# Segmented memory attention with a routed MLP: first step and tail rearranged, scratch layout of the left sums changed

## The chip, the cores and the metric

The kernel runs on one core of one Trainium2 chip. The metric is the device time of one launch in microseconds (us); less is better. The engines have short names: PE (matrix multiply, with PEld for its weight loads), DVE (vector), ACT (scalar), POOL (GpSimd) and SP (sync, which here only issues transfers). SBUF is the on-chip memory of 128 partitions, PSUM the small memory into which PE writes.

## The reference

x has 2048 rows of 1024, S = 64 segments of 32 rows; 32 heads of 128; F = 3584.

```python
xn = _layernorm(x)
mem = mem0                                      # 8 rows
for s in range(n_seg):
    xs = xn[:, s * seg_len:(s + 1) * seg_len, :]
    h = concatenate([mem, xs], axis=1)          # 40 rows
    q, k, v = h @ Wq, h @ Wk, h @ Wv            # 32 heads of 128
    p = softmax(where(mask, q @ k.T * E ** -0.5, -1e9))
    o = (p @ v) @ Wo                            # 40 rows of 1024
    mem = o[:, :M, :]                           # the next segment's memory
    outs.append(o[:, M:, :])
r = xn @ w_r; idx = argsort(-r)[:, :2]          # two routed rows
y = (silu(xn[idx] @ w_gate) * (xn[idx] @ w_up)) @ w_down * sigmoid(r[idx])
return x + concatenate(outs) + xn + scatter(y at idx)
```

## The kernel before

**Steps.** The 64 segments follow each other, since the memory of one is the output of the one before; each is a step. A segment of 40 rows is split into 32 *main* rows (8 memory and 24 own rows), whose products are made in its step, and 8 *left* rows, its last ones. The left rows need no memory for their q, k and v: the first step (s = 0) makes these for all segments at once (`left_qk`, `left_v`), with the matmul L500 into `PSG` and L527 into `PSV`, copies them into `GA` and `VG` and stores them to DRAM (`ql_d`, L519, and `vl_d`, L531). The later steps load their part back. The sums of the left rows (`OTL`) go to DRAM in every step (`ol_d`, stored by `store_sums`, L604) and are turned into output rows for all segments in the tail, by `load_left_out` (L595) and `left_rows_out` (matmul L874).

**Weights.** Wq, Wk, Wv and Wo are 64 granules of 512 KB, 0 to 47 in six phases of eight (Wq, Wk of heads 0 to 15, then of 16 to 31, then Wv), 48 to 63 Wo. 44 stay in SBUF (`wres`, `XLT`, `W8A`, `W8B`, `HP`), 3 are kept in PSUM, 17 are streamed in each step through five slots (`g`). A slot comes free when the matmuls on its granule are done. In the first step they come from the inputs; POOL's copies (`wsc`) are their source from step 1 on. Some resident granules come late, since their place first holds something else: `v_homes` are the places of Wv granules, and the last of them (`hx`) holds the router's scratch `XR` and the blocks `VG`.

**Phases of a step.** PE makes q and k of the main rows (L745), transposes them (L632), scores (L650, L652), after two more phases v, P V (L703, L706) and Wo (L798) into `WO`; DVE copies `WO` to `XN` (L828), which ends the step. In the first step, `left_qk` stands behind phases 0 to 3 and `left_v` behind 4 and 5.

**The router**, in the first step: row statistics on DVE (L238 to L242), square root on ACT (L243), `spread` on PE (L250) brings mean and scale of each row to its place, then `router_tile` for 16 tiles of 128 rows on DVE (L263, L265), and `router_out`, a top-2 over all rows, and the routed rows' numbers. `QKL` (L513), the first left q and k that the first step itself needs, is copied by DVE, then `KT` by ACT (L640) and DVE (L642).

**The tail.** `left_rows_out(0)`, `gate_up` for the first 20 of 32 pieces, `left_rows_out(1)`, `gate_up` for the rest, silu (L920), product (L922), the down matmuls (L930) into `YP`, and one sum (L933) with the two routed rows of the output. Since all rows of the output are stored without y before that, POOL loads these two rows back (L916) and SP stores them (L936), at row numbers that are read from memory. In `gate_up` each 128 x 128 block of w_gate or w_up is the stationary operand and the two rows (`RXT`) are the moving one: 14 blocks x 32 pieces = 448 matmuls with 2 columns.

**Order.** The program's order on each engine is the order in which the source writes it; an engine takes its instructions strictly in that order. SP and ACT share eight semaphore lanes for their transfers (DMAHW0 to 7), POOL has eight of its own (DMASW0 to 7); they are given out in turn, and a transfer waits for the one before it on its lane. Waits between instructions go by the tile that they read or write.

Of the kernel before, what the change touches and what calls it, by code (L numbers as in the profile page):

```python
# [22 lines left out]
KEPT_HERE = (FIRST_KEPT, NEXT_KEPT, HALF_KEPT)  # L23
NEG = -30000.0
# [5 lines left out]
def kernel(  # L30
# [29 lines left out]
    FH = F // 2  # L60
    SCALE = float(E) ** -0.5
# [56 lines left out]
    ol_d = [dram.tile([16, P, XL * H], BF16, name=f"ol_d{t}") for t in range(4)]  # L118
# [142 lines left out]
    def router_tile(t):  # L261
        XR = home(hx, [P, D], BF16, "XR")
        nc.vector.tensor_scalar(out=XR[:, :], in0=xt(t), scalar1=RI16[:, t, 0:1], scalar2=RI16[:, t, 1:2],  # L263
                                op0=ALU.subtract, op1=ALU.mult)
        nc.vector.tensor_tensor_reduce(out=XR[:, :], in0=XR[:, :], in1=WRB, scale=1.0, scalar=0.0,  # L265
                                       op0=ALU.mult, op1=ALU.add, accum_out=RF[:, t:t + 1])
# [155 lines left out]
    flow += [(s, g) for s in range(NSEG) for g in (streamed if s else first_streamed)]  # L422
# [6 lines left out]
    def fetch_moe(n=64):  # L429
        while moe and free_homes and n:  # L430
# [9 lines left out]
            else:  # L440
                nc.sync.dma_start(out=t.rearrange("p (a d) -> p a d", a=2),
                                  in_=B_w_down[2 * what[1] * P:(2 * what[1] + 2) * P, :].rearrange("(a p) d -> p a d", a=2))
# [35 lines left out]
    for g in range(KC, 32):  # L478
        if g in first_streamed:
# [6 lines left out]
    for g in v_homes[8:-1]:  # L486
# [6 lines left out]
    def left_qk(mat, half, Gs, between, h0=0, h1=16):  # L493
# [15 lines left out]
        if mat == 1:  # L509
# [3 lines left out]
            nc.vector.tensor_copy(out=qkl[0][:, half].rearrange("p m i q r -> p (m i q r)"), in_=G3[:, 0, :])  # L513
# [7 lines left out]
    def left_v(half, Gs):  # L521
        VG = home(hm, [P, 2048], BF16, "VG")
        for b in range(4):
            for jq in range(4):
                PSV = psA.tile([P, 512], F32, tag="acc", name="PSV")
                for kc in range(KC):
# [4 lines left out]
                nc.sync.dma_start(out=vl_d[b][4 * jq:4 * jq + 4, :, :, half, :].rearrange("i s r e -> (s r) i e"),  # L531
                                  in_=VQ.rearrange("p (i e) -> p i e", i=4))
# [15 lines left out]
    def left_done(p):  # L548
        for g in range(8 * p, 8 * (p + 1)):
            if g in first_streamed:  # L550
                fetch()
        if p == 1:
# [41 lines left out]
    def load_left_out(k, queue):  # L594
        queue.dma_start(out=areas["big0"][:, 4 * k:4 * k + 4, :], in_=ol_d[k // 4][4 * (k % 4):4 * (k % 4) + 4].rearrange("s p c -> p s c"))  # L595
# [6 lines left out]
    def store_sums():  # L602
        s, t = unsaved.pop(0)
        nc.gpsimd.dma_start(out=ol_d[s // 16][s % 16], in_=t.rearrange("p r h -> p (r h)"))  # L604
# [367 lines left out]
```

## Time and profile before

| | us |
|---|---|
| median of three runs | 1859.54 |
| lowest, highest | 1859.37, 1860.27 |
| the profiled execution | 1847.92 |
| its span | 1846.3 |
| first step, to the last copy of WO (L828) | 241.4 |
| 63 later steps, to 1760.3 | 1518.9 |
| tail | 86 |

Over the span PE is busy 84%, DVE 48%, ACT 42%, POOL 17%; 678.5 MB are moved at 367 GB/s in the mean. The table has three parts that are limited in different ways: the first step makes the left rows of all segments, the later steps each bring in 17 granules (8.9 MB), and the tail makes the left rows' outputs and the routed MLP. An order in time has a row for each run of like instructions: start, duration, engine, line, operation, out<-in, and in brackets the idle time of the engine before it and what ended it.

### The profile page before, as it was taken

To read this page: it belongs to the slowest core of one execution; us is meant where nothing else is said; L and a number is where in the kernel's file an instruction comes from. 1 tells how busy PE (TensorE), PEld (TensorE's weight loads), DVE (VectorE), ACT (ScalarE), POOL (GpSimd) and SP (SyncE) were. 2 spreads that over 40 slices of the span, in tenths; PEclk is the share of its full clock that TensorE was granted. 3 is DMA by queue.
4 is the path that set the end of the run, shared out by engine and by line. 5 is a ranking of instruction groups with operands and counts; after the bars stand their busy time and mean duration, and the time that the engine had idled before them with its cause. 6 is when DMAs were issued, how large, how long until landed. Compare 5 with 4: busy or idle time off the path is not lost. (4 is left out here: it accounts for less than half of the span.)

```text
span 1846.3 us, 70379 instructions
## 1 busy us (share of the span) xinstructions
PE 1555.7 (84%) x30358; PEld 828.2 (45%) x30370; DVE 880.4 (48%) x2711; ACT 774.9 (42%) x2019; POOL 320.9 (17%) x592
## 2 busy tenths in 40 slices
PE   6889978888888888888888888888888888888888
PEld 3334434444444444444444444444444444444465
DVE  6631235555554454555555555444455555555420
ACT  2333134444444444444444444444444444444400
POOL 1020111111111111111111111111111111111200
PEclk9999989999999999999999999999999999999988
DMA  9684899999999999999999999999999999999996
GB/s 361 218 301 135 261 367 391 393 394 394 368 387 376 368 389 383 392 386 372 396 393 396 396 394 394 385 386 389 386 391 394 397 382 393 395 395 395 392 364 251
DMA packets 223288, 678.50 MB, mean 367 GB/s; under 512 B 46848, under 2 KB 54320, under 8 KB 222976
## 3 DMA queue, kind: packets, MB, share of 16 engines
q1 hardware_dynamic: 196768, 623.79, 88.3%
q0 software_dynamic: 24192, 46.54, 7.5%
q8 instruction: 237, 3.88, 0.8%
q10 hardware_dynamic: 2016, 3.67, 0.6%
q14 instruction: 75, 0.61, 0.1%
HBM read 652.90 MB, written 29.89 MB: 370 GB/s over the span
## 5 line engine op out<-in xcount | busy, mean ns | idle before, releaser
L745 PE MATMUL PSm<-wres,ST 128*32 128x512 bf16 x6400 | 500.7, 382 | 0.0
L745 PEld LDWEIGHTS <-ST 128*32 128x32 bf16 x12288 | 313.3, 96 | 349.5 <-issue 107.4
L745 PE MATMUL PSm<-g,ST 128*32 128x512 bf16 x3084 | 307.3, 384 | 46.6 <-DMA g<-wsc 38.2
L411 ACT COPY BK<-KEPT 128x512 bf16<-128x512 bf16 x315 | 189.3, 601 | 175.0 <-PE WO L798 65.1
L798 PEld LDWEIGHTS <-OT 128*32 128x32 bf16 x8192 | 209.2, 97 | 85.6 <-issue 69.3
L754 ACT CAST XB<-PSm 128x512 bf16<-128x512 f32 x256 | 150.2, 587 | 132.7 <-PE PSm L745 131.1
L642 DVE COPY KT<-BT 128x512 bf16<-128x512 bf16 x128 | 51.8, 405 | 290.6 <-PE BT L632 290.6
L798 PE MATMUL WO<-W8B,OT 128*32 128x256 bf16 x4096 | 186.2, 276 | 0.0
L745 PE MATMUL PSm<-W8A,ST 128*32 128x512 bf16 x2048 | 182.7, 380 | 0.0
L587 POOL DMA_DIRECT2D QKL<-ql_d x63 | 46.5, 738 | 755.7 <-ACT OTL L714 740.6
L798 PE MATMUL WO<-g,OT 128*32 128x256 bf16 x2560 | 130.7, 277 | 53.1 <-DMA g<-wsc 48.8
L832 POOL DMA_DIRECT2D out_dram<-XN x256 | 130.7, 526 | 173.9 <-DVE XN L828 173.8
L779 ACT CAST VM<-PSm 128x512 bf16<-128x512 f32 x128 | 80.3, 627 | 114.0 <-PE PSm L745 114.0
L411 DVE COPY BK<-KEPT 128x512 bf16<-128x512 bf16 x189 | 80.2, 425 | 72.3 <-ACT BK L411 36.9
L632 PEld LDWEIGHTS <-XB 128*128 128x128 bf16 x1024 | 57.9, 98 | 106.6 <-ACT XB L754 101.5
L674 DVE TENSOR_REDUCE DN<-BS 128x8 f32<-128x320 f32 x128 | 62.9, 491 | 88.0 <-ACT BS L669 88.0
L632 PE MATMUL BT<-IDENT,XB 128*128 128x128 bf16 x1024 | 101.7, 222 | 3.1
L500 PE MATMUL PSG<-XLT,wres 128*128 128x512 bf16 x352 | 101.3, 390 | 0.8 <-ACT GA L502 0.7
L637 ACT COPY QT<-BT 128x512 bf16<-128x512 bf16 x128 | 74.9, 585 | 53.4 <-PE BT L632 51.4
L659 DVE TENSOR_TENSOR BS<-BS,CT 128x96 f32<-128x96 f32 (+1 forms) x256 | 59.7, 233 | 76.5 <-PE BS L652 72.0
L745 PE MATMUL PSm<-BK,ST 128*32 128x512 bf16 x567 | 76.7, 388 | 22.2 <-DVE ST L369 22.2
L828 DVE CAST XN<-WO 128x256 bf16<-128x256 f32 x64 | 27.2, 424 | 127.5 <-PE WO L798 127.5
(171 smaller groups left out, 2278.9 us busy)
## 6 DMA issues: line engine op xcount, KB each, us to landing
g<-wsc SPq DMA_DIRECT2D x1071, 512.0 KB, 6.3
ql_d<-GA POOLq DMA_DIRECT2D x16, 512.0 KB, 6.3
QKL<-ql_d POOLq DMA_DIRECT2D x63, 128.0 KB, 6.2
MW<-in_B_w_gate_dram SPq DMA_DIRECT2D x16, 448.0 KB, 8.0
MW<-in_B_w_down_dram SPq DMA_DIRECT2D x14, 512.0 KB, 8.3
wres<-in_A_Wk_dram SPq DMA_DIRECT2D x12, 512.0 KB, 10.5
MW<-in_B_w_up_dram SPq DMA_DIRECT2D x12, 448.0 KB, 8.5
XP<-in_A_x_dram SPq DMA_DIRECT2D x8, 512.0 KB, 10.1
```

The costliest lines, as they stand in the source:

```text
L411: copy(out=back[g][c], in_=KEPT_COLS[g][c])
L500: nc.tensor.matmul(PSG[:, :], lhsT=part(Gs[kc], h // 4)[:, P * (h % 4):P * (h % 4 + 1)], rhs=XLT[:, :, kc, :], start=(kc == 0), stop=(kc = ...
L632: nc.tensor.transpose(out=PTq[:, il, :, :].rearrange("p j r -> p (j r)"), in_=XB[:, il * P:(il + 1) * P], identity=IDENT[:, :])
L637: nc.scalar.copy(out=QT[half][:, :, :], in_=pv)
L642: nc.vector.tensor_copy(out=KT[half][:, :, 0:32], in_=pv)
L659: nc.vector.tensor_tensor(out=S4, in0=S4, in1=m, op=ALU.add)
L674: nc.vector.tensor_reduce(out=DN[:, :], in_=S8, axis=AX.X, op=ALU.add)
L745: nc.tensor.matmul(PSm[32 * jq:32 * jq + 32, :], lhsT=ST[:, kc, :], rhs=part(Gv, jq), start=(kc == 0), stop=(kc == KC - 1), tile_position= ...
L754: nc.scalar.copy(out=XB[:, :], in_=PSm[:, :])
L779: nc.scalar.copy(out=VM[half][:, :], in_=PSm[:, :])
L798: nc.tensor.matmul(PS[32 * g:32 * g + 32, 0:256], lhsT=lhs(h), rhs=Gv[:, D * hs + 256 * g:D * hs + 256 * (g + 1)], start=False, stop=(last ...
L832: nc.gpsimd.dma_start(out=out2[s * SEG:s * SEG + XM, 256 * g:256 * (g + 1)], in_=OB[32 * g:32 * g + XM, :])
```

## The change

It has five parts.

1. *Guest granule.* Granule 15 (phase 1) is loaded by SP among the first resident ones, into the place of granule `v_homes[8]`, and not into a stream slot; `v_homes[8]` itself is loaded after phase 1.
2. *Router.* Square root, `spread` and the 16 router tiles stand behind the left block of phase 0 instead of inside that of phase 1; `XR` has two buffers. The copies of `QKL`, and of `KT` in the first step, are made by ACT instead of DVE.
3. *Stores of v.* The stores of the last two left v blocks of half 1 are issued by POOL instead of SP.
4. *Layout of ol_d.* Partition first, segment second, so a store writes 512 B rows 8 KB apart, and a load of four segments reads 2 KB rows.
5. *Tail.* gate and up have the two rows, padded to 32 columns (`RX`), as the stationary operand and 448 columns of the weights as the moving one, in four column tiles: 128 matmuls. The result has rows of F over the partitions, so it is transposed (7 transposes) behind silu and product, and w_down is loaded in another row order. Silu's table is loaded ahead by an activation of one column. `keep_warm` puts 12 and 5 matmuls with no use into PE's pauses. The left rows' stores go to POOL (three) and SP (the last) instead of ACT, the two routed rows' stores to SP and ACT.

```diff
-    ol_d = [dram.tile([16, P, XL * H], BF16, name=f"ol_d{t}") for t in range(4)]
+    ol_d = [dram.tile([P, 16, XL * H], BF16, name=f"ol_d{t}") for t in range(4)]
...
+    def router_tiles():
+        XR = home(hx, [P, 2, D], BF16, "XR")
+        for t in range(NT):
+            nc.vector.tensor_scalar(
+                out=XR[:, t % 2, :], in0=xt(t), scalar1=RI16[:, t, 0:1], scalar2=RI16[:, t, 1:2],
+                op0=ALU.subtract, op1=ALU.mult)
...
-    moe += [("dn", fg) for fg in range(FC // 2)]
+    moe += [("dn", j, gp) for j in range(FC // 4) for gp in range(2)]
...
+        if g == GUEST:
+            t = res_tiles[g] = room(v_homes[8], "guest")
+            nc.sync.dma_start(out=t, in_=granule_dram(g))
...
-            nc.vector.tensor_copy(out=qkl[0][:, half].rearrange("p m i q r -> p (m i q r)"), in_=G3[:, 0, :])
+            nc.scalar.copy(out=qkl[0][:, half].rearrange("p m i q r -> p (m i q r)"), in_=G3[:, 0, :])
...
-                nc.sync.dma_start(out=vl_d[b][4 * jq:4 * jq + 4, :, :, half, :].rearrange("i s r e -> (s r) i e"),
-                                  in_=VQ.rearrange("p (i e) -> p i e", i=4))
+                (nc.gpsimd if half and b > 1 else nc.sync).dma_start(
+                    out=vl_d[b][4 * jq:4 * jq + 4, :, :, half, :].rearrange("i s r e -> (s r) i e"), in_=VQ.rearrange("p (i e) -> p i e", i=4))
...
     def left_done(p):
...
-        if p == 1:
+        if p == 0:
+            sd_rows(MV[:, 1:NT, :], VE[:, 1:NT])
+            spread(1, NT)
+            router_tiles()
+        elif p == 1:
+            res_tiles.pop(GUEST)
+            load_resident(v_homes[8])
...
-                nc.vector.tensor_copy(out=KT[half][:, :, 0:32], in_=pv)
+                (nc.vector.tensor_copy if s else nc.scalar.copy)(out=KT[half][:, :, 0:32], in_=pv)
...
-                        sd_rows(MV[:, 1:NT, :], VE[:, 1:NT])
-                        left_qk(mat, half, Gs, kept, 1, 3)
-                        h1 = 3
-                        spread(1, NT)
-                        for t in range(NT):
-                            router_tile(t)
...
+    def keep_warm(n):
+        W = psK.tile([P, 512], F32, name="WARM", tag="kept0")
+        for i in range(n):
+            nc.tensor.matmul(W[:, 0:256], lhsT=IDENT[:, :], rhs=T2[:, 256:512], start=True, stop=True)
...
-            nc.scalar.dma_start(out=out2.rearrange("(t s r) d -> t s r d", t=4, s=16)[2 * k + b, :, XM:SEG, :], in_=x)
+            (nc.sync if k and b else nc.gpsimd).dma_start(
+                out=out2.rearrange("(t s r) d -> t s r d", t=4, s=16)[2 * k + b, :, XM:SEG, :], in_=x)
...
-            for fl in range(FC // 2):
-                col = (w * FC + fh * (FC // 2) + fl) * 2
-                nc.tensor.matmul(GU[:, col:col + 2], lhsT=Gt[:, fl * P:(fl + 1) * P], rhs=RXT[:, kc, :],
-                                 start=(w + kc + fh + fl == 0), stop=True, skip_group_check=True)
+            for g in range(4):
+                nc.tensor.matmul(GU[w][fh][32 * g:32 * g + 32, 0:FQ], lhsT=RX[:, kc, :], rhs=Gt[:, FQ * g:FQ * (g + 1)],
+                                 start=(kc == 0), stop=(kc == KC - 1), tile_position=(0, 32 * g), skip_group_check=True)
...
-    SG = T2[:, 64:64 + 4 * FC].bitcast(F32)
-    nc.scalar.activation(out=SG, in_=GU[:, 0:FC * 2], func=ACTF.Silu)
-    HT = T2[:, 256:256 + 2 * FC].rearrange("p (f c) -> p f c", c=2)
-    nc.vector.tensor_tensor(out=HT.rearrange("p f c -> p (f c)"), in0=SG, in1=GU[:, FC * 2:FC * 4], op=ALU.mult)
+    HR = T0[:, 256:256 + 2 * FQ]
+    SG = [[T0[:, 1152 + 448 * i:1152 + 448 * (i + 1)].bitcast(F32) for i in range(2)],
+          [one.tile([P, 224], F32, tag=tag, name="SG") for tag in ("bA", "bE")]]
+    for fh in range(2):
+        for i in range(2):
+            nc.scalar.activation(out=SG[fh][i], in_=GU[0][fh][:, 224 * i:224 * (i + 1)], func=ACTF.Silu)
...
+    keep_warm(12)
+    HTP = psA.tile([P, 1024], BF16, tag="acc", name="HTP")
+    for j in range(FC // 4):
+        nc.tensor.transpose(out=HTP[:, P * j:P * (j + 1)], in_=HR[:, P * j:P * (j + 1)], identity=IDENT[:, :])
...
+    keep_warm(5)
...
-        v = nc.sync.value_load(I8[0:1, c:c + 1], min_val=0, max_val=S - 1)
-        nc.sync.dma_start(out=routed_out(v), in_=quarters(c))
+        ends[c].dma_start(out=routed_out(end_rows[c]), in_=quarters(c))
```

The first step on ACT, around the left block of phase 1 (`GA` is a left block's copy, `MISC` holds the row statistics, L243 is the square root), before:

```order
L502 CAST GA<-PSG 128x64x8 [waits PE_49] x2
L637 COPY QT<-BT 128x512 [waits PE_49]
L754 CAST XB<-PSm 128x512 [waits PE_49]
L502 CAST GA<-PSG 128x64x8 [waits PE_49]
L243 ACTIVATE MISC<-MISC 128x15 [waits DVE_49]
L502 CAST GA<-PSG 128x64x8 [waits PE_49] x15
L640 COPY KT<-QKL 128x16x8 [waits DVE_49,PE_49]
```

and in the change:

```order
L515 CAST GA<-PSG 128x64x8 [waits PE_49] x2
L245 ACTIVATE MISC<-MISC 128x15 [waits DVE_49]
L656 COPY QT<-BT 128x512 [waits DVE_49,PE_49]
L773 CAST XB<-PSm 128x512 [waits PE_49]
L515 CAST GA<-PSG 128x64x8 [waits PE_49] x16
L526 COPY QKL<-GA 128x256 [waits DMASW3_49,DMASW2_49,DMASW4_49,DMASW1_49,Activation_49]
L659 COPY KT<-QKL 128x16x8 [waits PE_49,Activation_49]
L661 COPY KT<-BT 128x16x32
```

The square root has moved ahead of the copy of phase 1's q, and the two copies ahead of the scores stand on ACT itself.

SP at the end of the first step, from the last v stores on, before (`XLT` and `wres` take resident Wo granules, `wsc` is the stream of step 1):

```order
L531 DMA vl_d_100<-VG 128x4x128 [waits DMAHW3_49,Activation_49]
L531 DMA vl_d_100<-VG 128x4x128 [waits DMAHW4_49,DVE_49]
L386 DMA g<-in_A_Wo_dram 128x2x1024 [waits DMAHW5_49,PE_49]
L386 DMA g<-in_A_Wo_dram 128x2x1024 [waits DMAHW6_49,PE_49]
L386 DMA g<-in_A_Wo_dram 128x2x1024 [waits DMAHW7_49,PE_49]
L136 DMA XLT<-in_A_Wo_dram 128x2x1024 [waits DMAHW0_49]
L136 DMA wres_2055<-in_A_Wo_dram 128x2x1024 [waits DMAHW3_49,DMAHW2_49,DMAHW4_49,DMAHW1_49,Pool_49]
L388 DMA g<-wsc_105 128x2048 [waits PE_49]
```

and in the change:

```order
L544 DMA vl_d_98<-VG 128x4x128 [waits DMAHW2_49,DVE_49]
L138 DMA XLT<-in_A_Wo_dram 128x2x1024 [waits DMAHW3_49,PE_49]
L559 DMA VL<-vl_d_97 128x1x128 [waits DMAHW6_49,DMAHW5_49,DMAHW4_49]
L390 DMA g<-in_A_Wo_dram 128x2x1024 [waits PE_49] x2
L390 DMA g<-in_A_Wo_dram 128x2x1024 [waits DMAHW7_49,PE_49]
L138 DMA XLT<-in_A_Wo_dram 128x2x1024 [waits DMAHW0_49]
L138 DMA wres_2040<-in_A_Wo_dram 128x2x1024 [waits DMASW3_49,DMASW2_49,DMASW4_49,DMASW1_49,DMASW7_49,DMASW0_49,DMAHW1_49,DVE_49,DMAHW2_49,Activation_49,Pool_49]
L392 DMA g<-wsc_105 128x2048 [waits PE_49]
```

Eight stores have left this place; the load into wres, whose place held VG, waits for the landings on POOL's lanes as well.

ACT in the tail, before (`T_39898` is T2, `GU` the sums of gate and up):

```order
L881 DMA out_dram<-XLS 16x8x1024 [waits DMAHW2_49,DVE_49]
L920 ACT_TABLE_LOAD [waits PE_49]
L920 ACTIVATE T_39898<-GU 128x56 [waits Activation_49]
```

and in the change (`T_39883` is T2, `T_39888` is T0, into which POOL loads the two routed rows on lanes DMASW2 and DMASW3):

```order
L935 ACT_TABLE_LOAD
L935 ACTIVATE T_39883<-T_39883 128x1 [waits Activation_49]
L942 TENSOR_LOAD CT [waits DVE_49]
L942 ISA x2
L948 ACTIVATE T_39888<-GA_40055 128x224 [waits DMASW3_49,DMASW2_49,PE_49]
L948 ACTIVATE T_39888<-GA_40055 128x224
L948 ACTIVATE SG<-GA_40056 128x224 [waits PE_49]
L948 ACTIVATE SG<-GA_40056 128x224
```

The first silu of the change waits for two of POOL's lanes besides PE.

More of the change, by code (lines that the diff above doesn't have):

```diff
@@ L23 @@
 KEPT_HERE = (FIRST_KEPT, NEXT_KEPT, HALF_KEPT)
+GUEST = 15
 NEG = -30000.0
@@ L60 @@
     FH = F // 2
+    FQ = F // 8
     SCALE = float(E) ** -0.5
@@ L485 @@
             load_x(g - 7)
-    for g in v_homes[8:-1]:
+    for g in v_homes[9:-1]:
         load_resident(g)
@@ L892, in routed_out @@
         return out2[bass.ds(v, 1), :].rearrange("o (g d) -> (o g) d", g=4)
-    GU = psA.tile([P, 512], F32, tag="acc", name="GU")
+    ends = (nc.sync, nc.scalar)
+    GU = [[psA.tile([P, 512], F32, tag="acc", name=f"GA{fh}") for fh in range(2)], [BS, BT]]
+    RX = T2[:, 256:512].rearrange("p (k r) -> p k r", r=32)
+    nc.vector.memset(T2[:, 256:512], 0.0)
+    nc.vector.tensor_copy(out=RX[:, :, 0:2], in_=RXT)
     pieces = [(w, kc, fh) for w in range(2) for kc in range(KC) for fh in range(2)]
```

52 lines of the change are left out of this document (31 added, 21 removed).

## The prediction

> **What bounds the kernel now.** I read the stretches of the span first, then the order in time of the engines in the two stretches that the change touches. The columns are the stretch, its length, busy time (and instructions) of PE, PEld, DVE, ACT and POOL, the granted clock, the DMA share and GB/s.
>
> ```profile
> 0.00:61.00 61.00, 40.51 (x284) 20.90 (x284) 37.77 (x97) 17.47 (x30) 4.75 (x19) 0.98 0.99 372
> 61.00:130.00 69.00, 62.27 (x341) 27.12 (x341) 34.85 (x66) 19.89 (x36) 12.38 (x24) 0.92 0.69 239
> 130.00:228.00 98.00, 92.37 (x567) 41.76 (x569) 21.38 (x47) 30.00 (x56) 15.54 (x30) 1.00 0.63 199
> 265.60:1737.00 1471.40, 1238.13 (x27402) 661.25 (x27406) 745.46 (x2383) 684.04 (x1835) 273.17 (x494) 1.00 1.01 389
> 1760.00:1846.00 86.00, 76.52 (x810) 52.16 (x814) 16.24 (x40) 2.99 (x4) 3.25 (x6) 0.86 0.86 307
> ```
>
> The middle, four fifths of the span, moves weights at a DMA share of 1.01: no compute saving shows there. From 61 to 228 us the DMA share is 0.63 to 0.69 and PE is busy nine tenths: there PE's waits set the time, and what they lose is lost for good, because every later step streams at a fixed rate. The tail from 1760 us is a chain on PE. So I price the first step and the tail as chains, the middle as bytes.
>
> **First step: guest granule and router.** Two stalls of PE stand in phases 1 and 2.
>
> ```profile
> 51.98 0.33 SPq L386 DMA_DIRECT2D g<-in_A_Wk_dram  x1
> 53.44 0.18 DVE L242 TENSOR_SCALAR MISC<-MISC 128x15 bf16<-128x15 bf16 x1
> 60.73 0.62 PE L745 MATMUL PSm<-g,ST 128*32 128x512 bf16 x4 [5.54 <-DMA g<-in_A_Wk_dram]
> 61.28 1.46 PE L500 MATMUL PSG<-XLT,wres 128*128 128x512 bf16 x3
> 65.39 0.22 ACT L243 ACTIVATE MISC<-MISC 128x15 bf16<-128x15 bf16 x1
> 69.80 0.45 DVE L263 TENSOR_SCALAR XR<-XP,MISC 128x1024 bf16<-128x1024 bf16 x1
> 97.54 0.55 DVE L263 TENSOR_SCALAR XR<-XP,MISC 128x1024 bf16<-128x1024 bf16 x1
> 78.01 0.81 PE L500 MATMUL PSG<-XLT,wres 128*128 128x512 bf16 x3
> 78.88 0.81 PE L500 MATMUL PSG<-XLT,wres 128*128 128x512 bf16 x3
> 91.06 1.05 PE L745 MATMUL PSm<-wres,ST 128*32 128x512 bf16 x16
> 99.58 0.30 ACT L640 COPY KT<-QKL 128x128 bf16<-128x128 bf16 x1 [7.83 <-DVE QKL L513]
> 99.93 0.23 PE L650 MATMUL BS<-KT,QT 128*32 128x40 bf16 x4 [6.73 <-ACT KT L640]
> 100.75 2.25 PE L500 MATMUL PSG<-XLT,wres 128*128 128x512 bf16 x5
> ```
>
> The first stall is granule 15: its load is issued at 51.98, when a stream slot comes free, and PE waits 5.54 us for it. Then PE runs at half pace for a while: three matmuls take 1.46 us, where from 78.01 to 78.88 four start in 0.87 (one of another tile stands between), 0.216 each. The left block after the stall lasts 29.8 us (61.28 to 91.06) against 27.6 at the steady pace (16 heads of 8, 128 x 0.216): 2.2 more. The guest loads the granule some 20 us sooner into a place that nobody reads before phase 4; the resident granule of that place is loaded after phase 1, at a DMA share of 0.69. What is not removed is the new place of spread: its four matmuls on PE wait for ACT's square root, which by 53.44 has its input but stands behind ACT's copy of a left block, and then runs at about 54.0; about 1.1 us of PE. Gain 5.54 + 2.2 - 1.1 = **6.6**.
>
> The second stall is the router on DVE: its 16 tiles start at 69.80 and come every 1.85 us ((97.54 - 69.80) / 15); the copy of QKL stands behind them, ACT waits 7.83 for it, PE 6.73 for ACT. Started at about 55.3 instead, the tiles end at 84.9, when phase 2 is just beginning at 84.5 (91.06 less the 6.6); its scores come about 2 us later, and the QKL and KT copies stand on ACT by now. The wait becomes the copies' own 0.25. With the half-paced start of the block behind it (the five at 100.75 take twice their 1.08, the four before them 0.35 too much: 1.4) the gain is 6.73 + 1.4 - 0.25 = **7.9**. The same KT copy on ACT costs 0.3 at phase 4. If the router's DVE work had no cover in phase 1's wait for data, its 29.6 us would have to stand somewhere else; DVE is busy 34.85 of 69 us there, so it has room.
>
> **First step: stores of the v blocks.**
>
> ```profile
> 215.07 14.52 SPq L531 DMA_DIRECT2D vl_d<-VG  x8
> 228.51 0.69 DVE L530 CAST VG<-PSV 128x512 bf16<-128x512 f32 x1 [3.82 <-DMA vl_d<-VG]
> 229.68 2.44 SPq L386 DMA_DIRECT2D g<-in_A_Wo_dram  x3
> 232.91 0.37 SPq L136 DMA_DIRECT2D wres<-in_A_Wo_dram  x1
> 234.04 0.62 PE L798 MATMUL WO<-g,OT 128*32 128x256 bf16 x8 [2.81 <-DMA g<-in_A_Wo_dram]
> 227.00:232.00 5.00, 3.79 (x92) 2.57 (x91) 2.68 (x11) 1.22 (x5) 0.39 (x2) 1.00 0.47 108
> 232.00:241.00 9.00, 4.63 (x66) 2.30 (x65) 0.44 (x2) 0.46 (x2) 0.50 (x1) 0.53 1.04 391
> ```
>
> Eight stores hold SP for 14.52 us, since each waits for its copy; three Wo granules, one more into XLT and the last resident one (wres) queue behind them. PE then waits 2.81, and less three times more, and the DMA share is 0.47 in 227 to 232. With the stores on POOL's queue the four granules can be issued about 5 us sooner. But wres goes where the VG blocks stand, so it still waits for the landing of POOL's last stores, and the stream of step 1 stands behind it on SP. POOL has only the eight W8B loads beside them. Lower bound: the idle DMA time of that stretch alone, 5 x 0.53 = 2.7 us. Upper: SP free at 223 to 224 instead of 229.6, about 6.5. Since wres can go only 1.5 us sooner, but finds the four loads done (2.1 MB, 5.4 us at 391 GB/s, half of it in idle time), I take **4**. First step in all: 6.6 + 7.9 - 0.3 + 4 = **18.2**, bounds 14 to 22.
>
> **Steady steps: layout of ol_d.** Each step stores 64 KB. Before, it was one contiguous block; now rows of 512 B stand 8 KB apart. The rows on q1 are those of 100 us of the steady part, of SP's loads of 512 B pieces (1787 to 1794), and of 1.5 us with 256 B stores (204.5 to 206).
>
> ```profile
> q1 hardware_dynamic: 10342, 37.66, 96.6%
> q1 hardware_dynamic: 2646, 2.39, 109.6%
> q1 hardware_dynamic: 1448, 0.37, 107.9%
> ```
>
> A big packet takes 0.966 x 16 x 100 / 10342 = 149 ns, a 256 B one 1.079 x 16 x 1.5 / 1448 = 18 ns. 64 KB are 16 big packets (2.4 us of engine time) or, at the worst of these, 256 small ones (4.6): 2.2 / 16 = 0.14 us a step, 8.6 in all. The mix of 512 B pieces moves 2.39 MB in 7.67 engine-shares-us against 37.66 in 96.6, which makes 0.21 instead of 0.17 us for 64 KB: 2.6 in all. I take **-3**, bounds -8.6 and 0. The loads of ol_d at the end get 2 KB rows instead; worth 0.5.
>
> **Tail.**
>
> ```profile
> 1790.02 1.28 DVE L880 TENSOR_TENSOR XLS<-XLS,WD 128x512 bf16<-128x512 bf16 x2 [10.84 <-PE WD L874]
> 1797.54 1.39 PE L903 MATMUL GU<-RXT,MW 128*128 128x2 bf16 x47 [1.31 <-issue]
> 1814.51 7.07 PE L874 MATMUL WD<-W8B,OTA 128*128 128x512 bf16 x32
> out_dram<-XLS ACTq DMA_DIRECT2D x4, 256.0 KB, 6.4
> T<-out_dram POOLq DMA_DIRECT2D x2, 2.0 KB, 2.5
> 1830.43 2.24 PE L903 MATMUL GU<-RXT,MW 128*128 128x2 bf16 x84
> 1832.75 1.28 ACT L920 ACT_TABLE_LOAD   x1 [58.68 <-PE GU L903]
> 1834.29 0.21 DVE L922 TENSOR_TENSOR T<-T,GU 128x56 bf16<-128x56 f32 x1 [4.55 <-ACT T L920]
> 1834.88 5.80 PE L930 MATMUL YP<-MW,T 128*2 128x256 bf16 x112 [2.22 <-DVE YP L924]
> 1835.79 1.21 POOL L916 DMA_DIRECT2D T<-out_dram  x2 [73.17 <-DMA out_dram<-XLS]
> 1840.74 0.48 DVE L933 SCALAR_TENSOR_TENSOR T<-YP,SIG,T 128x256 bf16<-128x256 f32 x1 [5.91 <-PE YP L930]
> 1835.00:1840.50 5.50, 5.50 (x112) 3.50 (x104) 0.00 (x0) 0.00 (x0) 1.21 (x2) 0.53 0.02 4
> ```
>
> The first pass of left rows ends at 1790.2. gate_up now needs RX, which DVE writes behind its adds: 1790.02 + 1.28, a memset and a copy of about 0.2 each, so it starts 1.5 us later than now. It then is 448-column matmuls in four column tiles, 0.19 us per group (the steady step runs four of 512 in 0.217): 20 groups 3.8, where 8.75 stood, 12 groups 2.3 for 4.2. The second pass of left rows runs 128 x 0.2155 = 27.6, without its slow start (29.55). The end of gate_up moves from 1832.7 to 1825.4, and the table load of 1.28 stands before it: **7.3 + 1.3 in hand**.
>
> I don't count it. The silu and its product now write into T0, the tile into which POOL loads the two routed rows, and both carry a wait for those two loads: other columns, but the wait is on the tile. Before, they wrote T2 and waited for nothing of the kind; only the last sum (L933) did. The rows can be loaded when all left rows are stored: the last adds end at 1824.5, the store lands 5.5 to 6.4 later (1830 to 1831), two issues (1.21) and a landing of 2.5 make about **1834**, where the silu ran at 1834.04 before. Behind it now stand four silus and products (1.6), seven transposes (0.4) and five warming matmuls at half pace (1.0), beside which the HT copy and the memset of YP run: 3.0 us, against 0.84 before (1834.04 to 1834.88). The down matmuls start at about 1837 instead of 1834.88. The pause that the 12 warming matmuls were to fill has grown to some 8 us, so PE is slow again and the 5.8 stay. Tail: -2.1 + 0.5 for ol_d, **-1.6**; bounds -4 and +1.
>
> The last row of the fence bears on that pace: in 5.5 us without a gap the clock is 0.53. The Trainium skill ("TensorE: Matmul & The Clock Gate", Part 1: The HAM clock gate) says that half rate follows an idle window of some 3.4 us and full rate some 3.4 us of sustained work. By that the five warming matmuls and the first down ones would release the clock and the down block would last about 4.1, an estimate; the trace disagrees, it has half pace for 5.5.
>
> **Sum.** 18.2 - 3 - 1.6 = 13.6 us. The profiled execution took 1847.92 with a span of 1846.3; the median of the runs is 1859.54, 11.6 above. 1847.9 - 13.6 = 1834.3, and with the same 11.6 **1845.9**. A difference under 0.2%, 3.7 us, would not be told from none.
>
> **Rivals.** (a) *The silu isn't held by the row loads*, because they land early or the wait is already met. For: the stores are spread over more queues. Then the silu runs at 1825.6, the down block from 1828.8 to 1834, and the row loads at 1834 end last: 1834 against 1842.5 for the last sum, 8 us better: 1838. Against: the landing times above. (b) *The stream of step 1 isn't advanced*: wres waits for POOL's stores, which land no sooner than SP's did, and what was won in the Wo phase is waited for in step 1. For: SP issues its stream strictly behind wres; DMA share 1.04 from 232. The 4 us are lost: 1849.9. (c) *Slower: the rows of ol_d 8 KB apart hold the DMA engines.* If each 512 B piece held an engine like a big packet (149 ns), a step's store would take 128 x 149 / 16 = 1.19 us instead of 0.15, 1.04 x 63 = 65 us: about 1914. It decides from (13.6 + 3) / 63 = 0.27 us a step, 52 ns a piece. Against: 256 B pieces at 18 ns. [...] (d) *The change doesn't do what it says in the first step*: the router's sums come early, but the chain to the top two rows has only about 1.6 us in hand before ACT's next square root, and PE waits there instead; or spread costs more. Some 5 us of the 18.2: 1851.
>
> **How the numbers follow.** My forecast 0.55, with an own range of 1842 to 1849; (a) 0.15; (b) 0.17; (d) 0.08; (c) 0.05. From (a) to (d), with the bounds of the steady steps, the range is 1836 to 1852.5. Faster by over 0.2% means under 1855.8: all cases but (c) and the far end of (d), 0.93; no difference 0.02; slower 0.05.
>
> **What would show it.** In the profile after: no wait of PE for granule 15 at phase 1, and a short one at spread; the router's tiles from 55 on; PE's wait for KT under 0.5 in phase 2; phase 2 beginning near 84.5; the end of the first step near 223; steps of 24.1 us and at most 0.1 more; gate_up in about 4 and 2.5 us; ACT's first silu waiting for the row loads until about 1834 less the gain, a PE pause of over 5 us ahead of the transposes, the down block at half pace. It would be wrong if the steps were longer by over 0.2 us, if the first step's end moved by less than 14, or if the silu followed gate_up at once.

## The result, and the profile after

| | before, us | changed, us |
|---|---|---|
| median (runs) | 1859.45 (4) | 1841.19 (4) |
| lowest to highest | 1858.11 to 1860.27 | 1834.65 to 1841.74 |
| profiled execution | 1847.92 | 1841.74 |
| its span | 1846.3 | 1840.0 |

The ratio of the runs is 0.9902, with a 95% interval of 0.988 to 0.9925: faster by 0.75 to 1.2%, 14 to 22 us. The forecast was 1845.9, 13.6 us less than before, in a range of 1836 to 1852.5. The two profiled executions, however, differ by 6 us only. Where these numbers part is seen by stage. First the stretches of the changed kernel's profile (columns as in the prediction):

```profile
0.00:61.00 61.00, 45.17 (x316) 23.41 (x316) 45.61 (x116) 19.80 (x35) 7.65 (x26) 1.00 1.00 373
61.00:115.00 54.00, 53.84 (x319) 24.00 (x317) 22.20 (x43) 18.88 (x34) 8.81 (x17) 1.00 0.80 276
213.00:226.00 13.00, 7.03 (x158) 4.21 (x156) 3.58 (x13) 1.91 (x7) 2.40 (x4) 0.83 0.84 303
226.00:1751.00 1525.00, 1279.65 (x28222) 683.14 (x28222) 766.75 (x2450) 703.10 (x1888) 282.23 (x511) 0.99 1.01 387
1751.00:1840.00 89.00, 71.80 (x528) 45.23 (x520) 17.95 (x46) 4.09 (x8) 4.88 (x9) 0.92 0.83 296
```

From 61 to 115 us PE has no gap left: 53.84 of 54 us, where it had 62.27 of 69 before, and the clock is full. The end of the first step (213 to 226) still has PE busy for 7 of 13 us. The middle moves its bytes at the same DMA share, 1.01, and 387 GB/s instead of 389. The tail is longer.

Now the copy of WO that ends each step, in the changed kernel and then in the kernel before, each with its count, durations in ns, and the first and the last start:

```profile
L841 DVE CAST XN<-WO x64: 424/425/426, 225.7 to 1751.3; 128x256 bf16<-128x256 f32 x64
```

```profile
L828 DVE CAST XN<-WO x64: 423/424/425, 241.0 to 1759.9; 128x256 bf16<-128x256 f32 x64
```

The first step ends 15.3 us sooner. The 63 steps behind it take 1525.6 us instead of 1518.9, which gives 6.7 back; the tail takes 88.7 (to 1840.0) instead of 86.4 and gives 2.3 back. 15.3 - 6.7 - 2.3 is the 6.3 us between the spans. So the question on the steps is whether those 6.7 us are the change's or this execution's, and that on the tail why work that became shorter ends later.

### The profile page after: what moved, and what is told of

Read it like the earlier page. It is cut to its first block, busy times and chain, and to the rows that moved or that the text cites. A ratio compares the mean times of both kernels' runs of the same rounds, so it can differ in the third digit from the quotient of the medians.

```text
span 1840.0 us, 69825 instructions
## 1 busy us (share of the span) xinstructions
PE 1550.2 (84%) x30074; PEld 821.4 (45%) x30074; DVE 879.7 (48%) x2713; ACT 778.2 (42%) x2027; POOL 326.5 (18%) x603
## 3 DMA queue, kind: packets, MB, share of 16 engines
q0 software_dynamic: 24816, 48.38, 7.8%
## 5 line engine op out<-in xcount | busy, mean ns | idle before, releaser
L764 PE MATMUL PSm<-wres,ST 128*32 128x512 bf16 x6400 | 501.1, 383 | 0.0
L764 PEld LDWEIGHTS <-ST 128*32 128x32 bf16 x12288 | 313.7, 96 | 341.0 <-issue 99.8
L764 PE MATMUL PSm<-g,ST 128*32 128x512 bf16 x3080 | 307.3, 385 | 41.3 <-DMA g<-wsc 38.0
L764 PE MATMUL PSm<-W8A,ST 128*32 128x512 bf16 x2048 | 182.7, 381 | 0.0
L764 PE MATMUL PSm<-BK,ST 128*32 128x512 bf16 x567 | 76.7, 390 | 22.2 <-DVE ST L373 22.2
## 6 DMA issues: line engine op xcount, KB each, us to landing
wres<-in_A_Wk_dram SPq DMA_DIRECT2D x12, 512.0 KB, 10.2
```

The source lines that it names most:

```text
L764: nc.tensor.matmul(PSm[32 * jq:32 * jq + 32, :], lhsT=ST[:, kc, :], rhs=part(Gv, jq), start=(kc == 0), stop=(kc == KC - 1), tile_position= ...
```

## The experiments

Each row is read from one profiled execution of its kernel: the start of the copy that ends the first step, the mean of the 63 steps (last less first start, over 63), and the tail (span less last start).

| kernel | first step ends | mean step | tail | median of runs (number) |
|---|---|---|---|---|
| before | 241.0 | 24.11 | 86.4 | 1859.45 (4) |
| before_again | 242.8 | 24.31 | 84.5 | 1850.42 (12) |
| changed | 225.7 | 24.22 | 88.7 | 1841.19 (4) |
| old_ol | 224.8 | 24.19 | 90.3 | 1842.96 (12) |
| own_row | 225.3 | 24.04 | 84.3 | 1839.57 (11) |
| own_row_pool | 226.2 | 24.31 | 83.6 | 1833.98 (6) |
| no_guest | 233.3 | 23.99 | 88.9 | 1835.03 (1) |
| router_back | 228.3 | 24.18 | 86.9 | 1840.43 (1) |
| v_on_sp | 227.9 | 24.06 | 88.0 | 1833.07 (1) |
| best1 | 230.5 | 24.21 | 78.1 | 1836.70 (6) |
| copies_dve | 226.4 | 24.35 | 89.0 | 1851.00 (1) |
| first_step_undone | 241.6 | 24.20 | 88.0 | 1855.99 (1) |
| rows_hw | 226.2 | 24.28 | 77.9 | 1829.95 (6) |
| best2 | 226.9 | 24.13 | 92.9 | 1842.72 (12) |

The versions ran in groups on different chips, on which the kernel before had medians of 1854.28 us (28 runs), 1852.98 (11) and 1857.47 (17). So medians of rows from different chips are not to be compared; the columns by stage can be.

**before_again**: no edit.

> The kernel before, unchanged, once more: what its runs differ by, and where the 11.6 us between its profiled execution (1847.9) and the median of its runs (1859.5) stand. Theory: they stand in the 63 streamed steps, whose mean was 24.11 us before and 24.22 in the changed kernel's execution, from stretches of steps of 25 to 26 us at different places; so a median of 1855 to 1860, a first step that ends at 241 +- 1, and a tail of 86 +- 1, while the steps' mean may lie between 24.1 and 24.3. Rival: the execution recorded before differed in its first step or its tail; then one of these two is off by several us.

Its median was 1850.42 (1840.44 to 1869.37), beside 1854.28 for 28 more runs of the same kernel on the same chip (1842.21 to 1866.45); the ratio of the kernel to itself was 0.9972, interval 0.994 to 1.0004. First step and tail agree with the first execution within 2 us, and the mean step does not: 24.11 and 24.31, 12.7 us over 63 steps. So the theory holds on the place, while first step and tail lie 1.8 and 1.5 us from the expected 241 and 86, where I had allowed 1, and the median was lower than I expected. Over all kernels of the table the mean step runs from 23.99 to 24.35 with no order in it, 23 us over 63 steps, where the first step repeats within 1 to 2 us. For this kernel a difference under some 5 us is therefore read by stage, and not from medians of a few runs.

**old_ol**: the layout of ol_d as before, in an otherwise changed kernel.

```diff
-    ol_d = [dram.tile([P, 16, XL * H], BF16, name=f"ol_d{t}") for t in range(4)]
+    ol_d = [dram.tile([16, P, XL * H], BF16, name=f"ol_d{t}") for t in range(4)]
```

> The changed kernel with the layout of ol_d as it was before (each step's sums one contiguous 64 KB). Theory from the trace of the changed kernel: the store still goes in packets of 4096 B (3741 on the software queue from 300 to 1700 us, 3744 before), so the layout costs the steps nothing and is worth some 0.5 to 1 us in the tail, where the loads move 2 KB instead of 512 B pieces: 0 to 2 us slower than the changed kernel, steps the same. Rival (the prediction's): the layout costs 0.05 us a step, and this kernel is 2 to 4 us faster than the changed one.

Mean step 24.19 against 24.22, ratio to before 0.9948 (0.9917 to 0.9979). More is told by the packets, here on POOL's queue from 300 to 1700 us (packets, MB, share of 16 engines), in the changed kernel and in this one:

```profile
q0 software_dynamic: 15819, 21.06, 4.5%
```

```profile
q0 software_dynamic: 15816, 21.06, 4.5%
```

With 58 steps in the stretch, pieces of 512 B would have made over 6000 more packets (128 for 16 in each step). There are three more, and over the whole program the queue has 24816 packets in both kernels. The strided store leaves as the same packets with the same share of time, so the layout does not cost the steps what I charged. (The mean steps, 24.19 and 24.22, could not show it: 3 us over 63 steps are lost in their scatter.) In the tail it seems worth more than the 0.5 I gave it: 90.3 here, against 86.9 to 89.0 in the six kernels with this tail and the new layout; that is one execution.

**no_guest**: granule 15 through a stream slot again.

```diff
-        if g == GUEST:
-            t = res_tiles[g] = room(v_homes[8], "guest")
-            nc.sync.dma_start(out=t, in_=granule_dram(g))
-        elif g in first_streamed:
+        if g in first_streamed:
...
-            res_tiles.pop(GUEST)
-            load_resident(v_homes[8])
```

> The changed kernel without the guest: granule 15 waits for a stream slot again. Read from the first step alone, since single executions of this kernel differ by 10 us in the streamed steps. Theory: PE waits 5 to 6 us for granule 15 in phase 1 and runs at half pace for some 4 us behind it, so phase 2 starts 7 to 8 us later than in the changed kernel and the first step ends at 232 to 234 instead of 225.8. Rival: the wait only moves work that later stalls hide (the end of the step waits for transfers), and the first step ends less than 4 us later.

PE in phase 1 of this kernel, in order of time:

```profile
53.78 0.25 PE L252 MATMUL BT<-MISC 128*128 128x30 bf16 x4 [0.81 <-ACT MISC L245]
61.44 0.62 PE L759 MATMUL PSm<-g,ST 128*32 128x512 bf16 x4 [5.23 <-DMA g<-in_A_Wk_dram]
```

The wait is back, and the first step ends 7.6 us later; the fourth later step still ends 5.3 later (329.9 against 324.6). The other row is the price of spread's new place, 0.8 us where I had put 1.1; it is paid in this kernel too, so the 7.6 are to be set against 5.54 + 2.2 = 7.7 of the forecast and not against its 6.6.

**router_back** and **copies_dve**: two edits that meet in PE's wait for KT, each undone alone; the first puts square root, spread and tiles back into the left block of phase 1, the second is

```diff
-            nc.scalar.copy(out=qkl[0][:, half].rearrange("p m i q r -> p (m i q r)"), in_=G3[:, 0, :])
+            nc.vector.tensor_copy(out=qkl[0][:, half].rearrange("p m i q r -> p (m i q r)"), in_=G3[:, 0, :])
...
-                (nc.vector.tensor_copy if s else nc.scalar.copy)(out=KT[half][:, :, 0:32], in_=pv)
+                nc.vector.tensor_copy(out=KT[half][:, :, 0:32], in_=pv)
```

> The changed kernel with square root, spread and router tiles back inside the left block of phase 1, but the copies of QKL and KT left on ACT. Theory: PE's wait in phase 2 was for the copies behind the router on DVE, and ACT does them now, so the wait does not come back in full: the scores run at once, and the first step ends at most 2 us later (226 to 228); so the copies on ACT are what won the 6.7 us, the router's place little. Rival (the prediction's): the router's place is what counts; DVE is busy with the tiles until about 93 when the scores need it at 85, and the first step ends 5 to 9 us later.

> The changed kernel with the copies of QKL and of KT in the first step back on DVE, the router staying early. With the router back in its old place and the copies on ACT the first step ended at 228.4 against 225.0 to 226.4 with both. Theory: either edit alone removes most of PE's 6.7 us wait, because in the changed kernel the tiles end at 81.6 and the copies stand behind nothing on either engine; so the first step ends at 225 to 227 here. Rival: the copies on ACT are what counts and on DVE they again come late; 229 to 233.

First step 228.3 and 226.4, against 225.7. With the router back, DVE is busy with the tiles to 90.5, but the scores start at once, since ACT has made the copies:

```profile
86.47 0.21 PE L665 MATMUL BS<-KT,QT 128*32 128x40 bf16 x4 [0.17 <-ACT KT L657]
```

So the two edits cover each other: either alone keeps PE from its 6.7 us wait. How much each brings is read from the starts of phases 2 and 3 on PE, between which that wait stood. Phase 3 of the kernel before, then phases 2 and 3 of the changed kernel, of router_back and of copies_dve:

```profile
129.74 0.83 PE L745 MATMUL PSm<-wres,ST 128*32 128x512 bf16 x12
82.89 1.05 PE L764 MATMUL PSm<-wres,ST 128*32 128x512 bf16 x16
113.75 0.83 PE L764 MATMUL PSm<-wres,ST 128*32 128x512 bf16 x12
84.17 1.05 PE L760 MATMUL PSm<-wres,ST 128*32 128x512 bf16 x16
115.03 0.83 PE L760 MATMUL PSm<-wres,ST 128*32 128x512 bf16 x12
82.88 1.05 PE L764 MATMUL PSm<-wres,ST 128*32 128x512 bf16 x16
113.41 0.83 PE L764 MATMUL PSm<-wres,ST 128*32 128x512 bf16 x12
```

Phase 2 began at 91.06 before, so this stretch took 38.7 us; it takes 30.9 in the changed kernel, 30.9 with the router back and 30.5 with the copies back. Each edit alone brings the whole gain here, and the other adds nothing to it. The 2.6 and 0.7 us at the end of the step arise outside this stretch: router_back begins phase 1 already 1.3 us later than the changed kernel (54.05 against 52.76). That start alone lies between 51.4 and 55.1 in the executions of the table, so 2 us at the end of a single first step say little.

**v_on_sp**: all v stores by SP again.

```diff
-                (nc.gpsimd if half and b > 1 else nc.sync).dma_start(
+                nc.sync.dma_start(
```

> The changed kernel with the stores of the last two v blocks back on SP. Theory: the stores on POOL gave nothing, since the load of wres waits 5.4 us for POOL's last landing (issued at 221.0 in the changed kernel, first load of the stream at 221.5); with the stores on SP the first load of the stream comes at 218 to 221.5, the first step ends at 225 to 227.5, and four steps later the two kernels are within 1.5 us. Rival (the prediction's): the stream comes 4 us later (225 to 226) and the first step ends at 229 to 230.

SP at the end of the first step, in the changed kernel, and in this one:

```profile
212.53 1.75 SPq L390 DMA_DIRECT2D g<-in_A_Wo_dram  x3
214.32 0.48 SPq L138 DMA_DIRECT2D XLT<-in_A_Wo_dram  x1
221.04 0.37 SPq L138 DMA_DIRECT2D wres<-in_A_Wo_dram  x1
221.46 17.86 SPq L392 DMA_DIRECT2D g<-wsc  x13
```

```profile
215.98 1.49 SPq L390 DMA_DIRECT2D g<-in_A_Wo_dram  x3
217.53 1.37 SPq L138 DMA_DIRECT2D XLT<-in_A_Wo_dram  x1
219.08 0.39 SPq L138 DMA_DIRECT2D wres<-in_A_Wo_dram  x1
219.52 20.54 SPq L392 DMA_DIRECT2D g<-wsc  x12
```

With POOL's help the Wo granules leave 3.5 us sooner, and wres and the whole stream 2 us later. The first step ends 2.2 us sooner, but the changed kernel began phase 1 2.0 us sooner, long before these stores (52.76 against 54.78). By the fourth later step nothing is left: 324.63 against 324.56. So the stores bring 2 us at most at the end of the first step and none behind it: rival (b) of the prediction is what happens.

**first_step_undone**: guest, router, copies and stores undone together; tail and ol_d of the change.

> The changed kernel with all three edits of the first step and the copies undone: its tail and its layout of ol_d alone. Theory: the first step ends where it does in the kernel before (241.1 and 242.8 in its two executions), the tail is that of the changed kernel (86.9 to 88.8) and so 1 to 3 us longer than before (84.5 and 86.3); the steps' mean is within the range of all executions so far (23.9 to 24.2 without the last). So the tail as written costs, and the whole gain is the first step's. Rival: the tail is shorter than before by itself and only the earlier first step spoils it; then a tail under 84.

First step 241.6, as before; tail 88.0. PE's wait for KT is 4.8 us here. So all of the gain is the first step's, and the tail as written costs. Over the six kernels of the table with this tail and the new layout it lasts 86.9 to 89.0, mean 88.3; over the two executions of before 85.5: 2.8 us.

**own_row**: the two routed rows in a tile of their own.

```diff
-    ROW = T0[:, 0:256]
+    ROW = one.tile([P, 256], BF16, tag="kt", name="ROW")
```

> The changed kernel with the two routed rows (ROW) in a tile of their own instead of in T0. Theory: the silu's 10.7 us behind gate_up are a wait on the tile alone; then the silu starts within 0.3 us of gate_up's end, the down matmuls run before the rows land, and the last sum waits for the rows instead (in the changed kernel's trace they land at 1827.1 and the sum is at 1834.8): 6 to 8 us faster than the changed kernel. Rival: the down matmuls wait for the last loads of w_down (the DMA falls idle at 1823.5) and run slowly behind a pause, so that less than 4 us are won.

The end of the changed kernel in order of time:

```profile
1814.94 0.61 SPq L899 DMA_DIRECT2D out_dram<-XLS  x1
1816.12 1.49 PE L884 MATMUL WARM<-T,IDENT 128*128 128x256 bf16 x12
1824.72 1.23 POOL L939 DMA_DIRECT2D T<-out_dram  x2 [22.80 <-DMA out_dram<-XLS]
1827.16 0.60 ACT L948 ACTIVATE T<-GA 128x224 f32<-128x224 f32 x2 [60.58 <-DMA T<-out_dram]
1828.00 1.29 PE L956 MATMUL HTP<-IDENT,T 128*128 128x128 bf16 x7 [10.39 <-DVE T L951]
1830.28 4.44 PE L967 MATMUL YP<-MW,T 128*2 128x256 bf16 x112
1834.77 0.48 DVE L970 SCALAR_TENSOR_TENSOR T<-YP,SIG,T 128x256 bf16<-128x256 f32 x1 [4.94 <-PE YP L967]
```

and of own_row:

```profile
1804.17 0.61 SPq L899 DMA_DIRECT2D out_dram<-XLS  x1
1805.35 0.68 DVE L951 TENSOR_TENSOR T<-T,BS 128x224 bf16<-128x224 f32 x2 [1.07 <-PE BS L925]
1807.83 3.23 PE L967 MATMUL YP<-MW,T 128*2 128x256 bf16 x112
1811.86 1.23 POOL L939 DMA_DIRECT2D ROW<-out_dram  x2 [20.71 <-DMA out_dram<-XLS]
1814.34 0.48 DVE L970 SCALAR_TENSOR_TENSOR ROW<-YP,SIG,ROW 128x256 bf16<-128x256 f32 x1 [6.57 <-DMA ROW<-out_dram]
1816.80 1.15 ACTq L972 DMA_DIRECT2D out_dram<-ROW  x1
```

In the changed kernel ACT's first silu is released by the row loads; PE's 12 warming matmuls end at 1817.6, and it then stands still for 10.4 us. With a tile of their own the rows hold nobody but the last sum: last left store to last sum is 10.2 us instead of 19.8. Yet the tail is only 4.4 us shorter, since the span ends 10.1 us behind that sum instead of 5.2. What stands there is on POOL, in the view of the program's last line (count, ns min/median/max, first and last start):

```profile
L1003 POOLq DRAIN  x3: 46/115/11073, 1812.5 to 1824.1; - x3
```

POOL drains 11.07 us behind its last transfer, the row loads. In the changed kernel the same 11.07 us ran from 1825.3, ended at 1836.4 and hid behind the last sum and its stores.

**own_row_pool**: also the last of the left rows' stores by POOL.

> As the kernel with ROW in its own tile, and the last of the four stores of left rows issued by POOL instead of SP. Theory: that store landed 9.8 us after its issue because it stood behind the loads of w_down on SP's queue; on POOL's it lands in 5 to 6.5, so the rows come 3 to 4 us sooner, and the end moves by up to 3 more: 9 to 11 us faster than the changed kernel, then limited by the last loads of w_down. Rival: the landing is slow because all DMA engines are full until 1822, whatever the queue; then no difference from the kernel with ROW in its own tile.

Tail 83.6, 0.7 less than own_row, not 3. The store did land sooner, 5.5 us behind its issue as expected, where it took 7.0 in own_row and 9.1 in the changed kernel. But the end is set by the drain by now: it starts behind POOL's row loads here too, at 1829.3, and lasts 11.16 us.

**best1**: own_row, and the row loads by SP and ACT behind the silu, the last left store by ACT, and wres by POOL.

```diff
+    for c in range(2):
+        ends[c].dma_start(out=quarters(c), in_=routed_out(end_rows[c]))
     keep_warm(12)
...
-            (nc.sync if k and b else nc.gpsimd).dma_start(
+            (nc.scalar if k and b else nc.gpsimd).dma_start(
...
-            for g in AREAS["pair"][1:] + [hm]:
+            for g in AREAS["pair"][1:]:
                 load_resident(g)
+            load_resident(hm, nc.gpsimd)
```

> The changed kernel with four edits: ROW in its own tile; the two routed rows loaded by SP and ACT behind the silu instead of by POOL; the last of the left rows' stores by ACT; the load of wres by POOL, so that the stream on SP does not stand behind it. Theory: the kernel with ROW in its own tile ended 10 us behind its last sum (1814.3 to 1824.4) because POOL's queue drains 11.1 us behind its last transfer, the row loads; with these on SP and ACT that ends before the last stores. Then the tail (from the last copy of WO to the end) is 77 to 80 us instead of 88.6 in the changed kernel and 84.1 with ROW alone. The stream of step 1 starts at 215 to 218 instead of 221.5. In all 10 to 13 us faster than the changed kernel: ratio to the kernel before 0.984 to 0.987. Rival: POOL's drain follows its last store of left rows all the same or the row loads on SP and ACT land later than POOL's, and the tail stays at 83 to 84.

The tail is 78.1, as expected. The first step is a miss: 230.5. PE in it:

```profile
229.44 0.62 PE L812 MATMUL WO<-wres,OT 128*32 128x256 bf16 x8 [5.40 <-DMA wres<-in_A_Wo_dram]
```

The stream left SP at 215.7, ahead of wres (222.3 on POOL), and PE waited 5.4 us for the one granule that this step still needed. From 216 to 224 the DMA share is 1.02, so wres, issued last, shared full DMA engines with that stream.

**rows_hw**: best1 with wres back on SP.

> The changed kernel with the three tail edits of the best version so far, and the load of wres on SP as in the changed kernel (on POOL it came 5.4 us late for PE: first step at 230.7). Theory: first step at 225 to 226.5, tail 77 to 79 (77.9 there), so 9 to 11 us faster than the changed kernel by stages; ratio to the kernel before 0.983 to 0.986. Rival: the tail's gain came from the later first step and shrinks to under 6.

First step 226.2, tail 77.9: 10.8 us shorter than in the changed kernel. Median 1829.95 (1823.61 to 1835.57), ratio to before 0.9833, interval 0.9793 to 0.9873. It has the lowest ratio of all versions here, and its interval lies below the changed kernel's, measured on another chip against the same kernel before. What ends last now, in order of time:

```profile
1826.25 1.36 ACTq L952 DMA_DIRECT2D ROW<-out_dram  x1
1827.81 0.39 PE L967 MATMUL YP<-MW,T 128*2 128x256 bf16 x8 [0.89 <-DMA MW<-in_B_w_down_dram]
1828.51 0.48 DVE L970 SCALAR_TENSOR_TENSOR ROW<-YP,SIG,ROW 128x256 bf16<-128x256 f32 x1 [4.83 <-DMA ROW<-out_dram]
```

The rows and the last of w_down come within a microsecond of each other.

**best2**: rows_hw, with RX written ahead of the first left rows, and the two blocks of w_down that go in as halves of 64 partitions loaded as transfers of 128 partitions, with an outer dimension of 2 in the source.

```diff
+                        src = bass.AP(tensor=B_w_down.tensor, offset=B_w_down.offset + r0 * D,
+                                      ap=[[(4 * FQ - P * j) * D, 2], [D, n0], [1, D]])
+                        nc.sync.dma_start(out=t3[:, a, :], in_=src)
```

> As that, and two more edits in the tail: RX written ahead of the first pass of left rows, so that gate_up need not wait 1.5 us for DVE; and the two blocks of w_down that were loaded as two transfers of 64 partitions each loaded as two transfers of all 128 partitions. Theory: the stretch of 5 to 7 us at 195 to 240 GB/s in the loads of w_down is those transfers of 64 partitions, so it goes and the loads keep 380 to 390 GB/s; they end 2 to 3 us sooner, the last store of left rows lands sooner, and with RX the tail is 3 to 4 us shorter than with the three edits alone: 74 to 75.5. Rival: the slow stretch has another cause (the row order of w_down in DRAM, or PE's reads), stays at about 220 GB/s, and only 1.5 us are won.

The first edit does what it should: gate_up starts without the 1.51 us for which it waits on DVE in rows_hw. But the tail grew to 92.9. Two stretches of it: ahead of those transfers, and in them.

```profile
1798.00:1801.00 3.00, 3.00 (x16) 1.97 (x15) 0.00 (x0) 0.00 (x0) 0.00 (x0) 1.00 1.06 391
1805.00:1811.00 6.00, 6.00 (x61) 3.58 (x62) 1.43 (x3) 0.00 (x0) 0.00 (x0) 1.00 0.14 53
```

A DMA share of 0.14 is some two of sixteen engines. The Trainium skill ("DMA: Bandwidth & Descriptors", Rules for kernel authors) has the rule that an outermost dimension of fewer than 16 entries keeps a whole transfer on at most as many engines; the trace agrees, with 2 of 16 = 0.125 beside its 0.14. I had asked about the slow stretch of the changed kernel's own loads, whose two rows follow: a full share at half the rate, in the place of the halves, against the loads after them.

```profile
1807.00:1814.00 7.00, 7.00 (x40) 4.45 (x42) 0.38 (x1) 0.00 (x0) 0.00 (x0) 1.00 1.07 220
1816.00:1820.00 4.00, 1.60 (x16) 1.09 (x12) 0.00 (x0) 0.00 (x0) 0.00 (x0) 1.00 1.05 385
```

Whether the halves of 64 partitions cause it stays open: best2 replaced one slow form by a slower one.

## Why the prediction came out as it did

The two waits in the first step and the held silu came as forecast; three other terms did not. By stages: first step 241.9 (mean of two) to 225.7, 16.2 us for 18.2 forecast; steps 0 for -3; tail -2.8 for -1.6; in all 13.4 for 13.6. The stages miss by 2, 3 and 1.2 us and cancel, so that the sums agree within 0.2 is luck.

The first step can be split by the starts of its phases on PE (first matmul of the main rows, L745 before and L764 after) and the start of the last copy of WO:

| on PE | before, us | changed, us | gain | forecast |
|---|---|---|---|---|
| start to phase 1 (spread) | 53.06 | 52.76 | 0.3 | -1.1 |
| phase 1 to 2 (guest) | 38.00 | 30.13 | 7.9 | 7.7 |
| phase 2 to 3 (router, copies) | 38.68 | 30.86 | 7.8 | 7.9 |
| phase 3 to 5 (KT on ACT) | 65.90 | 67.39 | -1.5 | -0.3 |
| phase 5 to the copy of WO (stores) | 45.35 | 44.58 | 0.8 | 4 |

Between executions of kernels that do the same there, the first row differs by up to 2.6 us and the fourth by 2, so their small terms aren't resolved.

- *Guest*: 7.7 forecast without spread, 7.9 by the phases; no_guest takes 7.1 us more than the changed kernel in the same stretch (7.6 at the end of its first step, 5.3 four steps later). Right, with the wait and the half-paced restart as put; the wait at spread is 0.8 instead of 1.1.
- *Router and copies*: 7.9 forecast, 7.8 by the phases. PE's wait for KT fell to 0.2 us (forecast 0.25). What the prediction missed is that one edit would have been enough: it let the tiles move and the copies move, and either alone takes the wait away.
- *Stores of v*: 4 forecast; 0.8 by the phases, 2 at most by v_on_sp, and 0 afterwards. The failing step is "I take 4": wres "can go only 1.5 us sooner" by my own working, and I let the stream gain more than that. It came 2 us later than with the stores on SP. (VG stands in the place of the last Wo granule, wres, and not in hx, as the description of the kernel has it.)
- *Layout of ol_d*: -3 forecast, 0 by the packets. The failing step is that rows of 512 B in DRAM make packets of 512 B; the packets did not change. I had bounded the price by small packets of other transfers, on SP's queue q1, and not looked at what the store sends on POOL's q0. Rival (c) falls with it.
- *Tail*: the mechanism held: silu behind the row loads, a PE pause of 10 us, warming that fills the wrong pause. Two sizes were off and partly cancel. The last store landed 9.1 us behind its issue (5.5 to 6.4 forecast), because it stood behind w_down on SP's queue. Eight kernels issue it there: it took 8 to 9.1 us in the six whose last load of w_down had left at most 2.3 us before, and 6.2 and 7.0 in the two where that lay 4 us back. On ACT's queue (best1, rows_hw) it took 6.8, although SP was issuing w_down at the same time. The down block took 4.4 us instead of 5.8. There I set the trace of before against the Trainium skill ("TensorE: Matmul & The Clock Gate", Part 1: The HAM clock gate), whose rule gave about 4.1. The rule was nearer. The granted clock in the changed kernel's profile, before and behind the switch:

```profile
1822.60:1832.80 10.20, 4.79 (x63) 2.78 (x66) 1.74 (x6) 1.10 (x4) 1.22 (x2) 0.50 0.01 4
1832.90:1839.00 6.10, 1.81 (x68) 1.26 (x56) 0.48 (x1) 0.00 (x0) 0.00 (x0) 1.00 0.01 3
```

  PE works from 1828.0 on and gets its full clock at about 1832.8, 4.8 us later. The same page of the Trainium skill also says that this window runs freely and doesn't start with the work. Worked out from that, an estimate: work that begins inside one window has to fill the next, so that between one and two windows pass, 3.4 to 6.8 us. That holds the 4.8 here and the 5.3 of the kernel before (from 1834.88 to 1840.2, where its granted clock goes from 0.54 to 1.00), which I took for a contradiction.
- *The time*: the median moved by 18.3 us, the stages by 13.4. More executions bear out the stages: the last copy of WO starts at 1766.9 us in the mean of three with the old first step (before, before_again, first_step_undone) and at 1750.2 in the mean of six with the new one whole (changed, old_ol, own_row, own_row_pool, rows_hw, best2). That is 16.7 us, and 13.9 with the tail's 2.8 taken off. Within those six it starts anywhere from 1740.1 to 1757.6, so streamed steps can move a median of four runs by the missing 5 us; that they did is not shown, and the interval of 14 to 22 us is that of four runs a side.

## What to carry to other kernels

A scratch tile that lends columns to two stages ties them together: before merging buffers, look for a late transfer into any column of the tile, and give that transfer a tile of its own. The queue of a transfer matters twice: what stands behind it in order, and, on POOL, what the engine still has to drain when the program could end. Where long streamed work makes runs differ by more than the change is worth, compare stages of profiles and not medians, and within a stage start at a mark just ahead of the edit.

## What was unexpected in the hardware's behaviour

POOL's drain at the program's end lasted 11.07 us behind its last transfers in the changed kernel and in own_row, and 7.64 in the kernel before; in rows_hw it ran from 1805.7, for 10.92 us, and cost nothing. Its length doesn't follow from POOL's transfers in the tail. Two kernels with the same three stores of left rows and the same row loads on POOL as the changed one, v_on_sp and old_ol:

```profile
L1003 POOLq DRAIN  x3: 46/115/7892, 1816.7 to 1831.1; - x3
L1003 POOLq DRAIN  x3: 46/115/2244, 1824.4 to 1839.0; - x3
```

The first sends the v stores of the first step by SP, the second has the old layout of ol_d; nothing else differs, and their drains are 3.2 and 8.8 us shorter. Why is open, and so is whether own_row would have ended sooner with the old layout.

A store into rows of 512 B, 8 KB apart, left in the same number of packets as a contiguous one.
